# The last two batches in three blocks of 512 tokens instead of four of 384, with PSUM and SBUF shared out anew

## The chip, the cores and the metric

The kernel runs on one core of a Trainium2 chip. The core has a matrix engine (TensorE, "PE" in the profile, with its weight loads as "PEld"), a vector engine (DVE), a scalar engine for activation functions (ACT), a general engine (POOL) and a sequencer that issues the transfers (SP). Matmul results land in PSUM, eight banks of 128 x 512 float32; everything else lives in SBUF. The metric is device microseconds of one execution, the median of several runs.

## The reference

Queries, keys and values have 4 batches, 8 heads, 768 positions and 64 dimensions per head. Each query attends to the keys less than 16 positions away, and to 24 pooled keys: the maximum of the keys over blocks of 32 positions, with log(32) added to their scores and the mean of the block's values as their value. The result, 3072 tokens x 512, goes through a gated feed-forward layer with 1536 hidden columns:

```python
k_sum = k.reshape(B, H, nb, block, D).max(axis=3)
v_sum = v.reshape(B, H, nb, block, D).mean(axis=3)
scores_l_m = np.where(mask_l, scores_l, -1000000000.0)
scores_all = np.concatenate([scores_l_m, scores_s], axis=-1)
a = softmax(scores_all)
x = a @ np.concatenate([v, v_sum], axis=2)       # 3072 x 512 after the heads are joined
out = (silu(x @ w_gate) * (x @ w_val)) @ w_out
```

The weights arrive as 64-bit floats; the kernel turns each into two parts, high and low, of the matrix engine's rounded float32.

## The kernel before

**Blocks.** The 3072 tokens are cut into eight blocks `k` of `TOK` = 384, two per batch, and the eight heads into four pairs `u`. Attention works on one unit (k, u) at a time, in tiles of 64 queries (`QT`): six of them, with windows of 96 keys and the 24 pooled ones, 120 columns (`KC`). The feed-forward layer works on one block and one slice `j` of 128 hidden columns at a time, twelve slices per block.

**One unit of attention.** `a_load` brings the keys of a batch (only in the batch's first block), the queries, the windows of keys (`kw`), and the values for pooling; `a_load_values` the windows of values (`vw`). `a_keys` takes the maximum over key blocks (DVE, L284) and copies it beside the windows (POOL, L154). `a_pool_values` sums the values (DVE, L305) and `a_values` turns the sum by a transpose (PE, L320), scales it (ACT, L321) and copies it beside the value windows (DVE). `a_scores` (L364) does the score matmuls into two PSUM banks, one per head of the pair. `a_exp` is a DVE step that adds the mask and finds the maximum (L408), and the exponential on ACT (L423) with its sum; `a_norm` divides (DVE L440, L441, then POOL L445). `a_transpose` turns the probabilities on PE (L460) and copies them out of PSUM (`pt`, by DVE and ACT). `a_out` multiplies them with the values (L487); `a_split` and `a_rest` cut the result into a high part `xh` (ACT) and a low part `xl` (DVE).

**One slice of the feed-forward layer.** `m_up` (L522) does the gate and then the val product, each as four pairs of heads times three terms (low weight x high input, high x low, high x high), 12 matmuls with 384 moving columns each, into one PSUM bank. `m_silu` (ACT, L528) reads the gate's bank, `m_mul` (DVE, L533) the val's. `m_high` and `m_low` split the product into `ah` (ACT) and `al` (POOL, L148). `m_down` (L572) has the product as weights and `w_o` as 512 moving columns: three terms for each 128 tokens, nine matmuls, accumulated over all twelve slices in one bank per 128 tokens. After the last slice each accumulator is copied to a tile `o` (three buffers) by ACT or DVE in turn and written out.

**Banks and buffers.** PSUM is shared out as two banks for gate and val (`psg`), three for attention (`ps3[0]`, the "a" banks; the first block's accumulators use them too), three for the accumulators (`ps3[1]`). Queries, windows, value windows and probabilities have two buffers each.

**Order.** The first two blocks, with the decoding of the weights, are a list written out by hand (`PROLOGUE`), and their order on each engine is fixed. From slice 6 of block 1 on, the order in the program is: gate, val, and the down product of the slice before. Between these lie numbered places, three per slice, in which the steps of the attention of the next block are put (`put_attention`), each step at a distance from the unit's own place, one unit per nine places. Instructions of this part are only tied to the end of the hand-written list: a planner, which simulates the engines, issues in the order of the program what its cost model holds ready, so a load, a reduction or a copy goes ahead of its written place where its buffer is free. In the trace PE keeps the written order there; loads and the reductions of keys run well ahead.

```python
        m_gate(k, j)
        do(3 * n)
        m_val(k, j)
        do(3 * n + 1)
        if prev:
            m_down(*prev)
        do(3 * n + 2)
```

Of the kernel before, what the change touches and what calls it, by code (L numbers as in the profile page):

```python
# [31 lines left out]
NBLK = B * HALVES  # L32
# [95 lines left out]
def body(ctx, tc, qP, kP, vT, vP, kq, q1, vE, vR, vO, wgv, wo, cst_in, out):  # L128
# [10 lines left out]
    stg = pool("stg", 2)  # L139
# [5 lines left out]
    ps3 = [pool(f"ps{i}", 3, space=bass.MemoryType.PSUM) for i in "ab"]  # L145
# [75 lines left out]
    banks = {"g": psg, "a": ps3[0], "b": ps3[1]}  # L221
# [4 lines left out]
    def a_load_keys(k, u):  # L226
        kt = stg.tile([P, PADS], F32, tag="stg", name=f"kt_{k}_{u}")
        nc.sync.dma_start(kt[:, :PADS], kP[k // HALVES, u])
        KT[u] = kt

    def a_load_queries(k, u):
        b, hf = divmod(k, HALVES)
# [11 lines left out]
    def load_second():  # L244

        t = pro.tile([P, NP, TOK], F32, name="q1")
        nc.sync.dma_start(t, q1)
        for u in range(NP):
            U.setdefault((1, u), {})["q"] = t[:, u]

    def a_load_windows(k, u):
        b, hf = divmod(k, HALVES)
        kw = att.tile([P, NT, KC], F32, tag="kw", name=f"kw_{k}_{u}")
        src = kP[b, u]
        nc.sync.dma_start(
            kw[:, :, :KW], bass.AP(src.tensor, src.offset + hf * TOK, [[PADS, P], [QT, NT], [1, KW]])
        )
        U.setdefault((k, u), {})["kw"] = kw

    def a_load(k, u):  # L260

        b, hf = divmod(k, HALVES)
        if hf == 0:
            a_load_keys(k, u)
        a_load_queries(k, u)
        a_load_windows(k, u)
        if hf == 0:
            vt = stg.tile([P, PADS], F32, tag="stg", name=f"vt_{b}_{u}")[:, :S]
            nc.sync.dma_start(vt, vT[b, u])
            VT[u] = vt  # L270

    def a_load_values(k, u):
        b, hf = divmod(k, HALVES)
        vw = att.tile([KC, NT, P], F32, tag="vw", name=f"vw_{k}_{u}")
        src = vP[b]
        nc.sync.dma_start(
            vw[:KW],
            bass.AP(src.tensor, src.offset + hf * TOK * DM + u * P, [[DM, KW], [QT * DM, NT], [1, P]]),
        )
        U.setdefault((k, u), {})["vw"] = vw  # L280

    def a_pool_keys(u):
        ks = one.tile([P, NB], F32, tag=f"ks{u}", name=f"ks_{u}")
        nc.vector.tensor_reduce(  # L284
            out=ks, in_=KT[u][:, WIN : WIN + S].rearrange("p (n j) -> p n j", j=BLK), axis=AX.X, op=ALU.max
        )
        ksum[u] = ks

    def a_join_keys(k, u):

        copy(
            "p",
            U[k, u]["kw"][:, :, KW:],
            ksum[u].rearrange("p (o n) -> p o n", o=1).broadcast_to([P, NT, NB]),
        )

    def a_keys(k, u):
        if k % HALVES == 0:
            a_pool_keys(u)
        a_join_keys(k, u)  # L300

    def a_pool_values(k, u):
        if k % HALVES == 0:
            vr = att.tile([P, NB], F32, tag="vr", name=f"vr_{k}_{u}")
# [8 lines left out]
    def a_values(k, u):  # L313

        b, hf = divmod(k, HALVES)
        if hf == 0:
            if u == 0:
                vsum["all"] = one.tile([KC, DM], F32, tag="vs", name=f"vs_{b}")
            pv = a_bank(k, u, "pv")
            nc.tensor.transpose(pv[:NB, :P], vsum[u], id_sb)  # L320
            nc.scalar.mul(vsum["all"][KW:, u * P : (u + 1) * P], pv[:NB, :P], 1.0 / BLK)  # L321
        copy("d", U[k, u]["vw"][KW:], pooled(u).broadcast_to([NB, NT, P]))
# [76 lines left out]
    def a_max(k, u, g):  # L399

        t = U[k, u]
        if g == 0:
            t["p"] = (att if k else pro).tile([P, NT, KC], F32, tag="p", bufs=2 if k else 3, name=f"p_{k}_{u}")
            t["nm"], t["sm"], t["ri"] = (sml.tile([P, NT], F32, tag=x, name=f"{x}_{k}_{u}") for x in ("nm", "sm", "ri"))
        for c in range(NT // 2):
            i = g * NT // 2 + c
            n = k % HALVES * NTP + c
# [3 lines left out]
                in1=bias_sb[:, 0 if n == 0 else 2 if n == HALVES * NTP - 1 else 1, :],  # L411
# [7 lines left out]
    def a_half_exp(k, u, g):  # L419
        t = U[k, u]  # L420
        for c in range(NT // 2):
            i = g * NT // 2 + c
# [20 lines left out]
    def a_scale(k, u):  # L443
        p, ri = U[k, u]["p"], U[k, u]["ri"]
        (nc.vector if on == "d" else nc.gpsimd).tensor_tensor(  # L445
            out=p,
            in0=p,
            in1=ri.rearrange("p (n o) -> p n o", o=1).broadcast_to([P, NT, KC]),
            op=ALU.mult,
        )  # L450
# [5 lines left out]
    def a_turn(k, u, g):  # L456
        ps = U[k, u][f"pp{g}"] = a_bank(k, u, f"pp{g}", on[:1] or "a")
        zeros(ps, on[1:])
        for c in range(NT // 2):
            nc.tensor.transpose(ps[:KC, c * P : (c + 1) * P], U[k, u]["p"][:, g * NT // 2 + c, :], id_sb)  # L460

    def a_turned(k, u, g):
        t = U[k, u]
        if "pt" not in t:
            t["pt"] = (one if k else pro).tile([KC, 2, TOK], F32, tag="pt", bufs=1 if k else 2, name=f"pt_{k}_{u}")
        copy(on or "da"[g], t["pt"][:, g, :], t[f"pp{g}"][:KC, :TOK])
# [6 lines left out]
    def a_out(k, u):  # L473
# [3 lines left out]
        for i in range(NT):  # L477
# [19 lines left out]
    def a_split(k, u):  # L497
        ps = U.pop((k, u))["xo"]
        xh = att.tile([P, TOK], F32R, tag=f"xh{u}", name=f"xh_{k}_{u}")
        xl = att.tile([P, TOK], F32R, tag=f"xl{u}", name=f"xl_{k}_{u}")  # L500
        copy(on or "a", xh, ps[:, :TOK])
        X[k, u] = (xh, xl, ps)

    def a_rest(k, u):
        xh, xl, ps = X[k, u]
        subtract("d", xl, ps[:, :TOK], xh)
# [5 lines left out]
    def m_up(k, j, nm, pairs=range(NP)):  # L512
# [5 lines left out]
        for u in pairs:  # L518
            xh, xl = X[k, u]
            cs = slice(u * P, (u + 1) * P)  # L520
            for n, (w, x) in enumerate(((wl, xh), (wh, xl), (wh, xh))):
                nc.tensor.matmul(  # L522
                    ps[:, :TOK], w[:, cs], x, start=u == 0 and n == 0, stop=u == NP - 1 and n == 2
                )

    def m_silu(k, j):
        a = mlp.tile([P, TOK], F32, tag="a", name=f"a_{k}_{j}")
        nc.scalar.activation(out=a, in_=A.pop(("g", k, j))[:, :TOK], func=AF.Silu)  # L528
        A[k, j] = a

    def m_mul(k, j):
        a, ps = A[k, j], A.pop(("v", k, j))
        nc.vector.tensor_tensor(out=a, in0=ps[:, :TOK], in1=a, op=ALU.mult)  # L533

    def m_high(k, j):
        a = A[k, j]
        ah = mlp.tile([P, TOK], F32R, tag="ah", name=f"ah_{k}_{j}")
# [3 lines left out]
    def m_low(k, j):  # L541
        ah, a = A[k, j]
        al = mlp.tile([P, TOK], F32R, tag="al", name=f"al_{k}_{j}")
# [19 lines left out]
    def m_down(k, j):  # L563
        if j == 0:
# [3 lines left out]
        for i in range(NTP):  # L568
# [6 lines left out]
            if j == NJ - 1:  # L575
                o = mlp.tile([P, DM], F32, tag="o", bufs=3, name=f"o_{k}_{i}")
                r = k * TOK + i * P

                parts = 2 if k == NBLK - 1 and i == NTP - 1 else 1
# [20 lines left out]
    def load_consts():  # L600
        nonlocal bias_sb, id_sb, mean_sb
        c = cst.tile([P, 3 * KC + P + NV * QC], F32, name="consts")
        nc.sync.dma_start(c, cst_in)
        bias_sb = c[:, : 3 * KC].rearrange("p (v c) -> p v c", v=3)
        id_sb = c[:, 3 * KC : 3 * KC + P]
        mean_sb = c[:, 3 * KC + P :].rearrange("p (v n) -> p v n", v=NV)
# [11 lines left out]
    def next_room(n):  # L618
        nonlocal pro
# [4 lines left out]
        else:  # L624
            close_pool("dec")
            wts.append(pool("wts3", 1, reuse_waits="tile"))

    bias_sb = id_sb = mean_sb = None
    dec = open_pool("dec", 2, side="right")
# [42 lines left out]
    outs = []  # L672

    def put_attention(k, places, **more):
        steps = dict(
            load=-8, load_values=-4, keys=-3, pool_values=-2, scores=0, exp=0, norm=2, values=2, transpose=4, out=5,
            split=5, rest=5,
        )
        for u, place in enumerate(places):
            for n, x in (steps | more).items():  # L680
                if k == 2 and u == NP - 1:
                    x -= n in ("transpose", "out", "split", "rest")

                if k > 2 and n in ("load", "keys", "pool_values", "scores", "exp"):
                    x += outs[-1] - place
                if (n, k, u) != ("load", 2, 0):
                    put(max(0, place + x), step[n], k, u)
                if n == "out":
                    outs.append(place + x)
# [74 lines left out]
```

## Time and profile before

| | us |
|---|---|
| median of 3 runs (709.41 to 709.81) | 709.42 |
| the profiled execution, its own time | 709.2 |
| its span, first to last instruction | 707.4 |
| PE busy | 701.9 |
| ACT busy | 308.0 |
| DVE busy | 281.7 |
| POOL busy | 137.0 |
| transfers, share of 16 engines' span | 26.2% |

The span is what the profile covers; the execution's own time is 1.8 us more. Engine rows give start and length in us, then engine, line, operation, output and inputs, shapes and count; what stands in square brackets or behind "idle" is how long the engine stood idle before and what ended it. Rows of grouped instructions give the group's busy time and the mean ns of one. A matmul's length holds its way through the array, so successive ones overlap; the distance of their starts tells what one costs. In the chain of waits each row is a start, a length, and the work on the chain.

### The profile page before, as it was taken

To read this page: it belongs to the slowest core of one execution; us is meant where nothing else is said; L and a number is where in the kernel's file an instruction comes from. 1 tells how busy PE (TensorE), PEld (TensorE's weight loads), DVE (VectorE), ACT (ScalarE), POOL (GpSimd) and SP (SyncE) were. 2 spreads that over 40 slices of the span, in tenths; PEclk is the share of its full clock that TensorE was granted. 3 is DMA by queue.
4 is the path that set the end of the run, shared out by engine and by line. 5 is a ranking of instruction groups with operands and counts; after the bars stand their busy time and mean duration, and the time that the engine had idled before them with its cause. 6 is when DMAs were issued, how large, how long until landed. Compare 5 with 4: busy or idle time off the path is not lost.

```text
span 707.4 us, 12740 instructions
## 1 busy us (share of the span) xinstructions
PE 701.9 (99%) x5116; PEld 639.8 (90%) x5116; DVE 281.7 (40%) x822; ACT 308.0 (44%) x765; POOL 137.0 (19%) x143
## 2 busy tenths in 40 slices
PE   9999999999999999999999999999999999999997
PEld 6799999998889999999999999999999999999997
DVE  6999899856642222232332122232223221210001
ACT  6975443327754434344444344443345442421111
POOL 2400120003322221222221222212222212211110
PEclk9999999999999999999999999999999999999999
DMA  9998001146642110222331211120111200010001
GB/s 343 343 419 340 1 1 54 50 136 200 181 141 68 45 45 25 89 68 69 91 88 64 52 45 45 45 90 6 41 46 45 90 18 1 1 45 0 1 1 44
DMA packets 48967, 61.58 MB, mean 87 GB/s; under 512 B 20956, under 2 KB 38108, under 8 KB 47628
## 3 DMA queue, kind: packets, MB, share of 16 engines
q1 hardware_dynamic: 48908, 60.77, 26.2%
q8 instruction: 40, 0.66, 0.4%
q14 instruction: 19, 0.16, 0.1%
HBM read 54.17 MB, written 6.29 MB: 85 GB/s over the span
## 4 chain that ended last, share of the span: by engine, by line
PE 99%; DMA 1%; DVE 0%; SPq 0%; ACT 0%; issue 0%
PE v L522 29%; PE g L522 29%; PE acc L572 28%; PE xo L487 4%; PE pp L460 3%; PE sc L364 3%; PE sc L394 1%; DMA kq<-in_kq 1%; PE sc L380 1%; PE xo L495 0%; PE sc L591 0%; PE pv L338 0%; PE pv L320 0%; PE sc L389 0%; DVE o L154 0%; SPq L240 0%
## 5 line engine op out<-in xcount | busy, mean ns | idle before, releaser
L522 PE MATMUL v<-xh,w_gv 128*128 128x384 f32 x640 | 179.6, 342 | 0.0
L572 PE MATMUL acc<-w_o,ah 128*128 128x512 f32 x576 | 178.9, 392 | 0.0
L522 PE MATMUL g<-xh,w_gv 128*128 128x384 f32 x640 | 178.6, 340 | 0.0
L533 DVE TENSOR_TENSOR a<-v,a 128x384 f32<-128x384 f32 x96 | 53.4, 556 | 252.6 <-PE v L522 250.1
L148 POOL TENSOR_TENSOR al<-a,ah 128x384 fp32r<-128x384 f32 x81 | 83.1, 1026 | 312.6 <-ACT ah L152 297.1
L572 PEld LDWEIGHTS acc<-w_o,ah 128*128 128x128 f32 x576 | 108.0, 188 | 19.9
L522 PEld LDWEIGHTS v<-xh,w_gv 128*128 128x128 f32 x640 | 117.1, 188 | 3.5 <-issue 2.4
L522 PEld LDWEIGHTS g<-xh,w_gv 128*128 128x128 f32 x640 | 117.3, 188 | 2.5 <-ACT a L528 0.4
L572 PE MATMUL acc<-w_o,al 128*128 128x512 f32 x288 | 113.6, 394 | 0.0
L528 ACT ACTIVATE a<-g 128x384 f32<-128x384 f32 x96 | 47.1, 490 | 148.6 <-PE g L522 144.7
L522 PE MATMUL g<-xl,w_gv 128*128 128x384 f32 x320 | 108.0, 338 | 0.0
L522 PE MATMUL v<-xl,w_gv 128*128 128x384 f32 x320 | 107.9, 337 | 0.0
L152 ACT CAST ah<-a 128x384 fp32r<-128x384 f32 x95 | 48.5, 511 | 122.5 <-DVE a L533 114.2
L423 ACT ACTIVATE p<-p,nm 128x120 f32<-128x120 f32 x192 | 73.3, 383 | 7.3 <-DVE nm L408 7.0
L445 POOL TENSOR_TENSOR p<-p,ri 128x720 f32<-128x720 f32 x31 | 43.4, 1400 | 110.6 <-DVE ri L441 105.9
L572 PEld LDWEIGHTS acc<-w_o,al 128*128 128x128 f32 x288 | 54.0, 188 | 9.5 <-issue 0.6
L522 PEld LDWEIGHTS g<-xl,w_gv 128*128 128x128 f32 x320 | 60.1, 188 | 2.2
L522 PEld LDWEIGHTS v<-xl,w_gv 128*128 128x128 f32 x320 | 60.1, 188 | 0.3
L528 ACT ACT_TABLE_LOAD x25 | 32.1, 1283 | 52.9 <-PE g L522 52.7
L408 DVE CUSTOM_DVE_ANT_0 p<-sc,consts 128x120 f32<-128x120 f32 x192 | 41.5, 277 | 2.1 <-PE pp L460 1.0
L522 PE MATMUL g<-xh,w_g 128*128 128x384 f32 x128 | 36.9, 343 | 0.0
L522 PE MATMUL v<-xh,w_v 128*128 128x384 f32 x128 | 36.8, 343 | 0.0
(94 smaller groups left out, 676.0 us busy)
## 6 DMA issues: line engine op xcount, KB each, us to landing
raw_gv<-in_wgv SPq DMA_DIRECT2D x10, 1024.0 KB, 14.6
kw<-in_kP SPq DMA_DIRECT2D x24, 288.0 KB, 3.9
vw<-in_vP SPq DMA_DIRECT2D x24, 288.0 KB, 3.3
raw_o<-in_wo SPq DMA_DIRECT2D x12, 512.0 KB, 13.8
out<-o SPq DMA_DIRECT2D x23, 256.0 KB, 2.3
kt<-in_kP SPq DMA_DIRECT2D x12, 400.0 KB, 3.7
q<-in_qP SPq DMA_DIRECT2D x24, 192.0 KB, 3.4
vt<-in_vT SPq DMA_DIRECT2D x12, 384.0 KB, 3.6
```

The source lines that it names most:

```text
L148: (nc.vector if e == "d" else nc.gpsimd).tensor_tensor(out=out, in0=a, in1=b.bitcast(F32), op=ALU.subtract)
L152: nc.scalar.copy(out, in_)
L364: nc.tensor.matmul(sc[h][s * QT : (s + 1) * QT, c * KC : (c + 1) * KC], t["q"][hs, qs], t["kw"][hs, i, :], start=True, stop=True,)
L408: nc.vector.tensor_tensor_reduce(out=t["p"][:, i, :], in0=t["sc"][g][:, c * KC : (c + 1) * KC], in1=bias_sb[:, 0 if n == 0 else 2 if n == ...
L423: nc.scalar.activation(out=t["p"][:, i, :], in_=t["p"][:, i, :], func=AF.Exp, scale=-1.0, bias=t["nm"][:, i : i + 1], accum_out=t["sm"][:, ...
L445: (nc.vector if on == "d" else nc.gpsimd).tensor_tensor(out=p, in0=p, in1=ri.rearrange("p (n o) -> p n o", o=1).broadcast_to([P, NT, KC]), ...
L460: nc.tensor.transpose(ps[:KC, c * P : (c + 1) * P], U[k, u]["p"][:, g * NT // 2 + c, :], id_sb)
L487: nc.tensor.matmul(ps[hs, qs], vw, t["pt"][:n, h, qs], start=k not in OWN or i == 0, stop=k not in OWN)
L522: nc.tensor.matmul(ps[:, :TOK], w[:, cs], x, start=u == 0 and n == 0, stop=u == NP - 1 and n == 2)
L528: nc.scalar.activation(out=a, in_=A.pop(("g", k, j))[:, :TOK], func=AF.Silu)
L533: nc.vector.tensor_tensor(out=a, in0=ps[:, :TOK], in1=a, op=ALU.mult)
L572: nc.tensor.matmul(ACC[k][i], a[:, ts], w, start=j == 0 and n == 0, stop=j == NJ - 1 and n == 2)
```

## The change

The first four blocks (batches 0 and 1) stay at 384 tokens. The other 1536 tokens become three blocks of 512: `SIZES` lists the widths, `START` the first tokens, and `parts_of(k)` tells which batches a block covers. Block 4 is the first 512 positions of batch 2, block 5 the rest of batch 2 and the first 256 positions of batch 3, block 6 the rest of batch 3. Loads and joins of pooled keys and values go by parts; batch 3 begins in the middle of block 5.

A wide block has eight tiles of 64 queries per unit, 512 columns in the up products, and four accumulators. PSUM: the three accumulator banks stay; when the first wide block begins its down products, the three attention banks are closed and become one bank for the fourth accumulator (`psx`) and two for attention (`psy`). For blocks 5 and 6 the second head's scores go to the two banks of gate and val. SBUF: keys, queries, windows, values, probabilities and their transposes of blocks 2 and up move to a pool `two`, opened where the decoding's buffers are closed, with two buffers for keys and pooled values and one for each of the others. The probabilities and transposes of block 1 move to the pool of the hand-written part. The places of block 2's units become 1, 5, 9 and 12 (they were 4, 7, 10, 13), and the distances of loads and joins are written out. The weights that pool the first batch's values move from the transfer of constants to the next one, that of block 1's queries.

```diff
+WIDE = 512
+NW = WIDE // QT
+SIZES = (TOK,) * (2 * HALVES) + (WIDE,) * ((B - 2) * S // WIDE)
+START = [sum(SIZES[:k]) for k in range(len(SIZES))]
+NBLK = len(SIZES)
+FIRST_WIDE = 2 * HALVES
...
+def parts_of(k):
+    found, at = [], START[k]
+    while at < START[k] + SIZES[k]:
+        b, pos = divmod(at, S)
+        n = min(S - pos, START[k] + SIZES[k] - at)
+        found.append((b, pos, (at - START[k]) // QT, n // QT))
+        at += n
+    return found
...
-    stg = pool("stg", 2)
...
-    ps3 = [pool(f"ps{i}", 3, space=bass.MemoryType.PSUM) for i in "ab"]
+    psb = pool("psb", 3, space=bass.MemoryType.PSUM)
...
-        q = att.tile([P, TOK], F32, tag="q", name=f"q_{k}_{u}")
-        nc.sync.dma_start(q, qP[b, u][:, hf * TOK : (hf + 1) * TOK])
+        q = two.tile([P, WIDE], F32, tag="q", name=f"q_{k}_{u}")
+        for b, pos, i, n in parts_of(k):
+            nc.sync.dma_start(q[:, i * QT : (i + n) * QT], qP[b, u][:, pos : pos + n * QT])
...
     def a_scores(k, u):
         t = U[k, u]
-        sc = [a_bank(k, u, f"sc{h}") for h in range(2)]
-        for i in range(NT):
+        sc = [a_bank(k, u, f"sc{h}", "ag"[h] if k > FIRST_WIDE else "a") for h in range(2)]
+        for i in range(SIZES[k] // QT):
...
         for u in pairs:
...
-                    ps[:, :TOK], w[:, cs], x, start=u == 0 and n == 0, stop=u == NP - 1 and n == 2
+                    ps[:, : SIZES[k]], w[:, cs], x, start=u == 0 and n == 0, stop=u == NP - 1 and n == 2
...
     def m_down(k, j):
+        m = SIZES[k] // P
         if j == 0:
-            ACC[k] = [ps3[1 if k else 0].tile([P, DM], F32, tag="b", name=f"acc{i}_{k}") for i in range(NTP)]
+            if k == FIRST_WIDE:
+                close_pool("psa")
+                banks["x"] = pool("psx", 1, space=bass.MemoryType.PSUM, reuse_waits="tile")
+                banks["a"] = pool("psy", 2, space=bass.MemoryType.PSUM, reuse_waits="tile")
+            ACC[k] = [
+                banks["x" if i == NTP else "b" if k else "a"].tile([P, DM], F32, tag="b", name=f"acc{i}_{k}")
+                for i in range(m)
+            ]
...
         else:
             close_pool("dec")
             wts.append(pool("wts3", 1, reuse_waits="tile"))
+            two = pool("two", 1, reuse_waits="tile")
...
-    def put_attention(k, places, **more):
+    def put_attention(k, u, place, **more):
         steps = dict(
-            load=-8, load_values=-4, keys=-3, pool_values=-2, scores=0, exp=0, norm=2, values=2, transpose=4, out=5,
+            load=-12, load_values=-4, keys=-7, pool_values=-6, scores=-4, exp=-4, norm=2, values=2, transpose=4, out=5,
             split=5, rest=5,
         )
...
-    put_attention(2, (4, 7, 10, 13), load=-5, load_values=-1)
+    early = dict(scores=0, exp=0)
+    put_attention(2, 0, 1, **early, load_values=-1, keys=-1, pool_values=-1)
+    put_attention(2, 1, 5, **early, load=-4, load_values=1, keys=-2, pool_values=-1, values=3)
+    put_attention(2, 2, 9, **early, load=-4, load_values=1, keys=-2, pool_values=-1, values=3, transpose=3)
+    put_attention(2, 3, 12, **early, load=-3, load_values=2, keys=-1, pool_values=0, values=4)
     for k in range(3, NBLK):
-        put_attention(k, [3 * NJ * (k - 2) - 18 + 9 * u + 1 for u in range(NP)])
+        for u in range(NP):
+            place = 3 * NJ * (k - 2) - 18 + 9 * u + 1
+            put_attention(k, u, place, **(dict(load=-7, keys=-5, scores=-2, exp=-2, load_values=-2) if (k, u) == (3, 0) else {}))
```

More of the change, by code (lines that the diff above doesn't have):

```diff
@@ L272, in a_load_values, with a_pool_keys @@
     def a_load_values(k, u):
[L273 to L279, printed above, removed]
+        vw = two.tile([KC, NW, P], F32, tag="vw", name=f"vw_{k}_{u}")
+        for b, pos, i, n in parts_of(k):
+            src = vP[b]
+            nc.sync.dma_start(
+                vw[:KW, i : i + n], bass.AP(src.tensor, src.offset + pos * DM + u * P, [[DM, KW], [QT * DM, n], [1, P]])
+            )
         U.setdefault((k, u), {})["vw"] = vw
-    def a_pool_keys(u):
+    def a_pool_keys(u, lead=WIN):
         ks = one.tile([P, NB], F32, tag=f"ks{u}", name=f"ks_{u}")
         nc.vector.tensor_reduce(
-            out=ks, in_=KT[u][:, WIN : WIN + S].rearrange("p (n j) -> p n j", j=BLK), axis=AX.X, op=ALU.max
+            out=ks, in_=KT[u][:, lead : lead + S].rearrange("p (n j) -> p n j", j=BLK), axis=AX.X, op=ALU.max
         )
         ksum[u] = ks
[L289 to L295, printed above, removed]
-    def a_keys(k, u):
-        if k % HALVES == 0:
-            a_pool_keys(u)
-        a_join_keys(k, u)
+    def a_keys(k, u):
+        for b, pos, i, n in parts_of(k):
+            if pos == 0:
+                a_pool_keys(u, 0)
+            copy(
+                "p",
+                U[k, u]["kw"][:, i : i + n, KW:],
+                ksum[u].rearrange("p (o n) -> p o n", o=1).broadcast_to([P, n, NB]),
+            )
     def a_pool_values(k, u):
-        if k % HALVES == 0:
-            vr = att.tile([P, NB], F32, tag="vr", name=f"vr_{k}_{u}")
+        if any(pos == 0 for b, pos, i, n in parts_of(k)):
+            vr = two.tile([P, NB], F32, tag="vr", name=f"vr_{k}_{u}")
             nc.vector.tensor_reduce(
@@ L313, in a_values @@
     def a_values(k, u):
[L315 to L322, printed above, removed]
+        for b, pos, i, n in parts_of(k):
+            if pos == 0:
+                if u == 0 and i == 0:
+                    vsum["all"] = one.tile([KC, DM], F32, tag="vs", name=f"vs_{b}")
+                pv = a_bank(k, u, "pv")
+                nc.tensor.transpose(pv[:NB, :P], vsum[u], id_sb)
+                nc.scalar.mul(vsum["all"][KW:, u * P : (u + 1) * P], pv[:NB, :P], 1.0 / BLK)
+            copy("d", U[k, u]["vw"][KW:, i : i + n], pooled(u).broadcast_to([NB, n, P]))
     def v_rows():
@@ L401, in a_max @@
         t = U[k, u]
+        m = SIZES[k] // P
         if g == 0:
[L403 to L407, printed above, removed]
+            if k < HALVES:
+                t["p"] = pro.tile([P, NT, KC], F32, tag=f"p{k}", bufs=3 - k, name=f"p_{k}_{u}")
+            else:
+                t["p"] = two.tile([P, NW, KC], F32, tag="p", name=f"p_{k}_{u}")[:, : 2 * m]
+            t["nm"], t["sm"], t["ri"] = (
+                sml.tile([P, NW], F32, tag=x, name=f"{x}_{k}_{u}")[:, : 2 * m] for x in ("nm", "sm", "ri")
+            )
+        for c in range(m):
+            i = g * m + c
+            n = (START[k] // P + c) % (S // P)
             nc.vector.tensor_tensor_reduce(
@@ L420, in a_half_exp @@
         t = U[k, u]
-        for c in range(NT // 2):
-            i = g * NT // 2 + c
+        for i in range(g * SIZES[k] // P, (g + 1) * SIZES[k] // P):
             nc.scalar.activation(
@@ L458, in a_turn @@
         zeros(ps, on[1:])
-        for c in range(NT // 2):
-            nc.tensor.transpose(ps[:KC, c * P : (c + 1) * P], U[k, u]["p"][:, g * NT // 2 + c, :], id_sb)
+        m = SIZES[k] // P
+        for c in range(m):
+            nc.tensor.transpose(ps[:KC, c * P : (c + 1) * P], U[k, u]["p"][:, g * m + c, :], id_sb)
     def a_turned(k, u, g):
@@ L464, in a_turned @@
         if "pt" not in t:
-            t["pt"] = (one if k else pro).tile([KC, 2, TOK], F32, tag="pt", bufs=1 if k else 2, name=f"pt_{k}_{u}")
-        copy(on or "da"[g], t["pt"][:, g, :], t[f"pp{g}"][:KC, :TOK])
+            if k < HALVES:
+                t["pt"] = pro.tile([KC, 2, TOK], F32, tag=f"pt{k}", bufs=2 - k, name=f"pt_{k}_{u}")
+            else:
+                t["pt"] = two.tile([KC, 2, WIDE], F32, tag="pt", name=f"pt_{k}_{u}")
+        copy(on or "da"[g], t["pt"][:, g, : SIZES[k]], t[f"pp{g}"][:KC, : SIZES[k]])
     def a_transpose(k, u):
@@ L476, in a_out @@
         n = KW if k in OWN else KC
-        for i in range(NT):
+        for i in range(SIZES[k] // QT):
             for h in range(2):
@@ L618, in next_room @@
     def next_room(n):
-        nonlocal pro
+        nonlocal pro, two
         if n == 0:
@@ L626, in next_room @@
             wts.append(pool("wts3", 1, reuse_waits="tile"))
+            two = pool("two", 1, reuse_waits="tile")
     bias_sb = id_sb = mean_sb = None
+    banks["a"] = open_pool("psa", 3, space=bass.MemoryType.PSUM)
     dec = open_pool("dec", 2, side="right")
@@ L670, in put @@
         at.setdefault(place, []).append((f, *a))
-    outs = []
-    def put_attention(k, places, **more):
+    def put_attention(k, u, place, **more):
         steps = dict(
-            load=-8, load_values=-4, keys=-3, pool_values=-2, scores=0, exp=0, norm=2, values=2, transpose=4, out=5,
+            load=-12, load_values=-4, keys=-7, pool_values=-6, scores=-4, exp=-4, norm=2, values=2, transpose=4, out=5,
             split=5, rest=5,
         )
[L679 to L689, printed above, removed]
-    put_attention(2, (4, 7, 10, 13), load=-5, load_values=-1)
+        for n, x in (steps | more).items():
+            if (n, k, u) != ("load", 2, 0):
+                put(place + x, step[n], k, u)
+    early = dict(scores=0, exp=0)
[3 more added lines that the diff above has]
+    put_attention(2, 3, 12, **early, load=-3, load_values=2, keys=-1, pool_values=0, values=4)
     for k in range(3, NBLK):
-        put_attention(k, [3 * NJ * (k - 2) - 18 + 9 * u + 1 for u in range(NP)])
+        for u in range(NP):
+            place = 3 * NJ * (k - 2) - 18 + 9 * u + 1
+            put_attention(k, u, place, **(dict(load=-7, keys=-5, scores=-2, exp=-2, load_values=-2) if (k, u) == (3, 0) else {}))
     def do(place):
@@ L750 @@
         "wo": np.ascontiguousarray(wo.reshape(NJ, P, DM)),
-        "consts": np.concatenate([x.reshape(P, -1) for x in (score_bias(), np.eye(P, dtype=np.float32), value_pool())], axis=1),
+        "consts": np.concatenate([x.reshape(P, -1) for x in (score_bias(), np.eye(P, dtype=np.float32))], axis=1),
     }
```

77 lines of the change are left out of this document (39 added, 38 removed).

## The prediction

> **What bounds the kernel now.** I read the page first (busy time per engine and the 40 slices), then the list of what TensorE (PE) waited for, then the chain of waits.
>
> ```profile
> span 707.4 us, 12740 instructions
> ...
> PE 701.9 (99%) x5116; PEld 639.8 (90%) x5116; DVE 281.7 (40%) x822; ACT 308.0 (44%) x765; POOL 137.0 (19%) x143
> ...
> PEclk9999999999999999999999999999999999999999
> ```
> ```profile
> PE warm L591 <- DVE warm L632: 1.4, 1, 1.4
> PE sc L380 <- DMA kq<-in_kq: 0.2, 1, 0.2
> ```
>
> The second fence is all that PE waited for: 1.6 us at the very start. Of the span, 707.4 - 701.9 = 5.5 us is not PE: those 1.6 us and a tail of 3.9 us. Since the page warns that a busy PE need not be at its peak, I looked at the distances from one matmul to the next. In the last block, which has no attention beside it, the chain of waits restricted to that stretch repeats one pattern per 128 hidden columns (start us, us, what):
>
> ```profile
> 645.00 2.11 PE g L522 x12
> 647.11 2.11 PE v L522 x12
> 649.22 2.08 PE acc L572 x9
> ...
> 688.97 2.12 PE g L522 x12
> 691.09 2.12 PE v L522 x12
> 693.21 2.04 PE acc L572 x9
> 695.25 2.12 PE g L522 x12
> ```
>
> From 645.00 to 695.25 there are eight patterns: 50.25 / 8 = 6.28 us each. The nine down matmuls (512 columns) take 2.04 to 2.08 us, 2.06 in the middle, so 229 ns each; the 24 up matmuls (384 columns) take the remaining 4.22 us, 176 ns each. The straight line through the two has (229 - 176) / 128 = 0.414 ns per column and 17 ns that do not depend on the columns. So the kernel is a queue of PE instructions without holes at a granted clock of 1.00, and the only ways to change its time are a different amount of PE work, a hole that opens in it, or its two ends.
>
> **The change part by part.**
>
> *Up projections (L522).* Per block there are 12 x 2 x 4 x 3 = 288 up matmuls, whatever its width. The last 1536 tokens have 4 x 288 = 1152 of 384 columns now and will have 3 x 288 = 864 of 512. The trace has no up matmul of 512 columns. From above, its cost is bounded by pure proportion, 176 x 512/384 = 235 ns; the nearest row is the down matmul, with the same 512 columns, 128x128 weights and three terms, at 229 ns; from below by 227 ns (2.04 us / 9). 1152 x 0.176 = 202.8 us becomes 864 x 0.229 = 197.9 us: -4.9 us, with -6.6 and +0.3 as bounds. The middle of the rows is uncertain by 1 ns, which is 0.9 us here, and I take -4.6. The down projection keeps its count: three matmuls of 512 columns per 128 tokens and 128 hidden columns.
>
> A rule of the Trainium skill (TensorE: Matmul & The Clock Gate, section "Wait — 56ns, not 53.3ns?") speaks against this term: it gives back-to-back matmuls N / 2.4 GHz plus only about 2.5 ns. By it 288 fewer matmuls would be worth 288 x 2.5 ns = 0.7 us. It would put 512 columns at 215.8 ns, and the down rows above have 229 ns, so the trace does not agree with its constant in this stream of paired weight loads.
>
> *Attention on PE.* A unit (one pair of heads of one block) is 6 transposes, 24 output and 24 score matmuls now, 8, 32 and 32 in a wide block. One unit in PE's timeline, and two points four units apart in the chain (same place of the pattern):
>
> ```profile
> 404.26 0.82 PE L460 MATMUL pp<-consts,p 128*120 128x128 f32 x6
> 404.83 0.42 PE L522 MATMUL g<-xh,w_gv 128*128 128x384 f32 x1
> 405.09 0.34 PE L522 MATMUL g<-xl,w_gv 128*128 128x384 f32 x1
> ...
> 407.12 0.92 PE L487 MATMUL xo<-pt,vw 120*64 120x64 f32 x24
> 407.97 0.85 PE L364 MATMUL sc<-kw,q 64*64 64x120 f32 x24
> 408.74 0.44 PE L522 MATMUL v<-xh,w_gv 128*128 128x384 f32 x1
> ```
> ```profile
> 387.43 2.31 PE v L522 x12
> 472.86 2.31 PE v L522 x12
> ```
>
> A block with four units beside it takes 85.43 us against 12 x 6.28 = 75.4: 2.5 us per unit. By the starts, six transposes take 0.57 us, 24 outputs 0.85, 24 scores 0.77, together 2.19; the other 0.3 us is the slower matmul at each change of kind (the first g after the transposes starts 0.26 us before the next, not 0.176). If everything but that 0.3 grows by a third, a wide unit is 2.5 + 0.73 = 3.23 us; twelve of them are 38.8 against sixteen old ones at 40.0: -1.2. But the 0.57, 0.85 and 0.77 hold a fixed part of their own, since a last matmul's drain is in each; with all of it fixed but the bare steps in between, I estimate some 3.1 us and -2. I take -1.6, bounds 0 (all proportional) and -2.2.
>
> *The end.* A wide block ends with four output tiles, and the pool of `o` still has three buffers, so the fourth copy must wait until the first tile has gone out.
>
> ```profile
> 702.25 0.59 ACT L152 COPY o<-acc 128x512 f32<-128x512 f32 x1 [1.54 <-PE acc L572]
> ...
> 702.86 2.11 SPq L583 DMA_DIRECT2D out<-o  x4
> 702.93 0.69 DVE L154 COPY o<-acc 128x512 f32<-128x512 f32 x1 [1.63 <-PE acc L572]
> ...
> 703.61 0.37 ACT L152 COPY o<-acc 128x256 f32<-128x256 f32 x1 [0.77 <-PE acc L572]
> ```
> ```profile
> DMA to landing us min/median/max: 2.0/2.0/2.1
> ```
>
> Copies of one accumulator follow the next at 0.68 us (702.25, 702.93, 703.61), three matmuls of 229 ns. The first copy ends 0.59 us after its start and its transfer lands 2.0 later: 2.65 us after the start with the issue. The fourth accumulator would be copied 3 x 0.68 = 2.04 us after the first. So the last copy starts about 0.7 us late: +0.7 (0.5 to 1.0). In the earlier wide blocks the same wait falls on ACT or DVE while PE goes on with the next block's ups, two of them at 12 x 0.229 = 2.75 us before an accumulator is wanted again.
>
> *Work that I cost at nothing, and its cover.* Silu, product, casts and subtraction grow by a third in columns and occur a quarter less often; the constants' table of pooling weights moves from one early transfer to the one after it, with the same bytes in front of everything later. The tightest chain is in the block before the first wide one: wide attention (eight exponentials) beside a 384 pattern of 6.28 us. The unit at 408 on the other engines:
>
> ```profile
> 407.29 0.49 ACT L528 ACTIVATE a<-g 128x384 f32<-128x384 f32 x1 [1.69 <-PE g L522]
> ...
> 408.58 1.28 ACT L423 ACT_TABLE_LOAD   x1
> ...
> 415.37 1.28 ACT L528 ACT_TABLE_LOAD   x1 [2.71 <-PE g L522]
> ```
> ```profile
> 412.84 1.39 POOL L445 TENSOR_TENSOR p<-p,ri 128x720 f32<-128x720 f32 x1 [3.60 <-DVE ri L441]
> 414.18 1.01 POOL L148 TENSOR_TENSOR al<-a,ah 128x384 fp32r<-128x384 f32 x1
> ```
> ```profile
> L423 ACT ACTIVATE p<-p,nm 128x120 f32<-128x120 f32 x192 | 73.3, 383 | 7.3 <-DVE nm L408 7.0
> ...
> L408 DVE CUSTOM_DVE_ANT_0 p<-sc,consts 128x120 f32<-128x120 f32 x192 | 41.5, 277 | 2.1 <-PE pp L460 1.0 <-PE sc L394 0.5 <-PE sc L364 0.3
> ```
>
> `al` is done at 415.2 and wanted by the down matmuls that follow val (408.74), down, gate and val: 408.74 + 2.2 + 3 x 2.1 = 417.2. Slack 2.0 us. Two more exponentials are 2 x 73.3 / 192 = 0.76, a third of the normalisation 0.46: 0.8 us of slack is left, and if it is gone, `al` late stops PE for the difference, at most four times. In the wide blocks the pattern is 3 x 2.75 = 8.25 us, and the slack is larger.
>
> *Shared PSUM banks.* From the second wide block on, one score bank comes out of the two that gate and val alternate in. The scores are issued right after a gate, so the val behind them needs the gate's bank back, that is, the silu. Cover: silu took 0.49 (0.65 at 512 columns), while the outputs and scores between take 0.85 + 0.77 plus a third, 2.1 us. The next gate needs the scores read by DVE, eight steps of 41.5 / 192 = 0.22 us, and comes two groups (5.5 us) later. Cost 0; without the outputs as cover, see the third rival.
>
> *The second batch's attention*, moved ahead, with one buffer instead of two for queries, windows, values and probabilities. A load can only start when the scores before it are done.
>
> ```profile
> kw<-in_kP SPq DMA_DIRECT2D x7, 288.0 KB, 4.3
> ```
> ```profile
> 160.00 0.85 PE L364 MATMUL sc<-kw,q 64*64 64x120 f32 x24
> ...
> 182.60 0.92 PE L487 MATMUL xo<-pt,vw 120*64 120x64 f32 x24
> ...
> 197.44 0.92 PE L487 MATMUL xo<-pt,vw 120*64 120x64 f32 x24
> ```
> ```profile
> 199.14 2.30 PE g L522 x12
> ```
>
> Scores to next scores is then at least 4.3 us of landing plus some 1 us of issue, and the 0.85 of the scores: 6.2. The first scores move up by a gate and a val (4.2 us) to about 155.8, so the fourth could come at 155.8 + 3 x 6.2 = 174.4. The order puts them in the place where the third unit's outputs stand now, near 182.6. The probabilities' buffer turns once per read by DVE (six times 0.22), table load (1.28), six exponentials (2.3), scaling (1.4) and transposes (0.6), with the hand-overs some 7.5 us, so the fourth scores can come at 155.8 + 22.5 = 178.3. So both chains fit; I take 0, bounds -0.5 (three of the transposes now stand beside scores and save a change of kind) and +4.
>
> **Sum:** -4.6 - 1.6 + 0.7 = -5.5 on the profiled execution, 709.2 us with its span of 707.4: 703.7. The median shown is 709.42, 0.2 above, so 703.9; I say 704.0.
>
> **The rivals.**
>
> 1. *The fixed 17 ns do not belong to the instruction.* If an up matmul costs by its columns alone (235 ns), the first term is gone: 709.4 - 1.6 + 0.7 = 708.5. For it: no up row of 512 columns exists. Against it: up and down have the same form and lie on one line with the same offset. The Trainium skill's constant of 2.5 ns, named above, would give nearly this: 707.8.
>
> 2. *Holes in the second batch.* The single buffers make the four units slip, and the first gate of that block, which needs all four, waits: the last unit's outputs came at 197.44 and the gate at 199.14. A slip of 1 us per unit costs up to 3 us after the small slack: 707. For it: loads and the reductions on keys share DVE with the products that release val's bank. Against it: the 4 us and more of slack above.
>
> 3. *The other side: the gate's bank is missed in every unit of the last two blocks' attention.* Eight units. If the planner issues scores without the outputs before them, or the silu there has to load its table first (1.28, as at 415.37), val waits for 1.28 + 0.65 + latency - 1.0 of scores, about 1 us, and all that follows with it: 8 us, 704.0 + 8 = 712. It decides from 5.5 / 8 = 0.7 us per unit. For it: two banks for three users. Against it: the silu at 407.29 has no table load ahead of it, because the one before it brought the table back.
>
> **How the numbers follow.** A change under 0.2% (1.4 us) cannot be told from none here. Forecast 0.65, first rival 0.07, second (with partial holes of other kinds, 705.5 to 708) 0.19, third 0.09. The likeliest one's own range is 702.3 to 705.5 by the bounds of its terms; taking in the second, 702.3 to 707.6. Faster: the forecast, most of the second, and a part of the first, 0.87; within 0.2%: 0.05; slower 0.08.
>
> **What would show it.** 864 up matmuls with 512 columns in the last blocks, twelve of them in 2.75 us (2.82 under the first rival); PE's list of waits as short as before; a block with wide attention of 99 + 12.5 us; a last copy of `o` that waits for a transfer. A wait of PE for ACT's silu or DVE's scores after 400 us speaks for the third rival, one near 199 us or before it for the second; waits of over 3 us in sum would make the prediction wrong.

## The result and the profile after

| | before | changed |
|---|---|---|
| median of runs on the same chip, us | 709.41 (709.28 to 709.81, 4 runs) | 701.38 (701.05 to 701.71, 4 runs) |
| profiled execution: its own time, us | 709.2 | 701.71 |
| its span, us | 707.4 | 699.9 |

The ratio is 0.9886 (95% interval 0.9869 to 0.9903): 8.0 us faster. The forecast was 704.0 with a range from 702.3 to 707.6; the time lies 0.9 us below that range. The profiled spans differ by 7.5 us only: the profiled execution of before lies 0.2 us under its median, that of the changed kernel is the longest of its four runs. The account below is one of the spans.

From the page of the changed kernel (the span; busy time, share and instructions of TensorE, PE; the granted clock in 40 slices):

```profile
span 699.9 us, 12044 instructions
...
PE 694.0 (99%) x4828; PEld 600.5 (86%) x4828; DVE 278.3 (40%) x795; ACT 292.1 (42%) x724; POOL 134.0 (19%) x127
...
PEclk9999999999999999999999999999999999999999
```

The list of what PE waited for has one row (total, times, longest, in us):

```profile
PE warm L623 <- DVE warm L665: 1.5, 1, 1.5
```

So it is what it was, a queue of PE instructions without holes at the full granted clock, with 288 fewer of them (5116 - 4828). The chain of waits in the last block, where no attention runs beside (start, duration, what):

```profile
592.11 2.72 PE acc L604 x12
594.83 2.72 PE g L546 x12
597.55 2.72 PE v L546 x12
600.27 2.72 PE acc L604 x12
...
690.02 3.42 PE acc L604 x15
```

Every group of twelve takes 2.72 us. From 592.11 to 690.02 there are twelve patterns of 36 matmuls: 97.91 / 432 = 226.6 ns each, up and down alike. The pattern of before was 6.28 us, and four of those did the work of three of these: 25.1 us have become 24.5.

**Where the time went.** One row of the stage windows each, first of before, then of the changed kernel (stretch; its length and the busy time of PE, then PEld, DVE, ACT and POOL; clock; DMA share; GB/s). They are cut at the first gate of block 2, at the first gate of block 4 (the first wide one) and at the end of the last matmul:

```profile
199.10:370.30 171.20, 171.20 (x1233) 157.40 (x1229) 50.46 (x186) 77.19 (x197) 37.04 (x41) 1.00 0.25 71
370.30:703.57 333.27, 333.27 (x2222) 308.00 (x2220) 69.71 (x245) 120.17 (x288) 67.39 (x69) 1.00 0.12 35
```
```profile
200.50:374.30 173.80, 173.80 (x1312) 159.82 (x1309) 53.81 (x205) 81.44 (x217) 39.08 (x42) 1.00 0.28 79
374.30:695.46 321.16, 321.16 (x1854) 264.72 (x1852) 65.39 (x203) 99.54 (x228) 62.62 (x52) 1.00 0.12 36
```

And from the chain the first scores of block 1 and the first gate of block 0, before and changed:

```profile
9.24 0.66 PE sc L380 x24
...
33.48 0.72 PE g L522 x3
```
```profile
9.87 0.66 PE sc L395 x24
...
34.11 0.73 PE g L546 x3
```

| stretch | before | changed | difference |
|---|---|---|---|
| start to the first gate of block 0 | 33.5 | 34.1 | +0.6 |
| to the first gate of block 2 | 165.6 | 166.4 | +0.8 |
| blocks 2 and 3 | 171.2 | 173.8 | +2.6 |
| the last 1536 tokens | 333.3 | 321.2 | -12.1 |
| last matmul to the end of the span | 3.8 | 4.4 | +0.6 |
| sum | 707.4 | 699.9 | -7.5 |

The +2.6 are the four wide units of attention that now run beside block 3 in place of narrow ones. In the last stretch 48 patterns of 6.28 us (301.4) became 36 of 8.16 (293.8): -7.7 for the products alone. What remains of the -12.1, that is -4.4, is attention, and with the +2.6 all attention of the last two batches comes to -1.8. One wide unit in the chain:

```profile
387.55 2.72 PE acc L604 x12
390.28 0.87 PE pp L481 x8
391.15 2.75 PE g L546 x12
393.90 1.08 PE xo L511 x32
394.98 0.98 PE sc L379 x32
395.96 2.95 PE v L546 x12
398.91 2.72 PE acc L604 x12
```

From one acc to the next are 11.36 us, so the unit takes 11.36 - 8.16 = 3.20; twelve of them make 38.4 us, against 40.0 for the sixteen narrow ones of 2.5.

### The profile page after: what moved, and what is told of

It is laid out like the page before. It is cut to its first block, busy times and chain, and to the rows that moved or that the text cites. A ratio compares the mean times of both kernels' runs of the same rounds, so it can differ in the third digit from the quotient of the medians.

```text
span 699.9 us, 12044 instructions
## 1 busy us (share of the span) xinstructions
PE 694.0 (99%) x4828; PEld 600.5 (86%) x4828; DVE 278.3 (40%) x795; ACT 292.1 (42%) x724; POOL 134.0 (19%) x127
## 4 chain that ended last, share of the span: by engine, by line
PE 99%; DMA 0%; ACT 0%; DVE 0%; issue 0%; DVEq 0%
PE v L546 29%; PE g L546 29%; PE acc L604 28%; PE xo L511 4%; PE pp L481 3%; PE sc L379 3%; PE sc L395 1%; PE sc L409 1%; PE warm L623 0%; PE xo L519 0%; PE sc L623 0%; DMA out<-o 0%; PE pv L353 0%; PE sc L404 0%; PE pv L335 0%; ACT o L168 0%
## 5 line engine op out<-in xcount | busy, mean ns | idle before, releaser
L546 PE MATMUL v<-xh,w_gv 128*128 128x384 f32 (+1 forms) x560 | 169.5, 363 | 0.0
L546 PE MATMUL g<-xh,w_gv 128*128 128x384 f32 (+1 forms) x560 | 168.4, 361 | 0.0
L557 DVE TENSOR_TENSOR a<-v,a 128x384 f32<-128x384 f32 (+1 forms) x84 | 51.6, 614 | 250.6 <-PE v L546 242.2
L164 POOL TENSOR_TENSOR al<-a,ah 128x512 fp32r<-128x512 f32 (+1 forms) x69 | 80.7, 1170 | 310.3 <-ACT ah L168 298.9
L552 ACT ACTIVATE a<-g 128x384 f32<-128x384 f32 (+1 forms) x84 | 45.1, 537 | 156.0 <-PE g L546 152.1
L546 PE MATMUL g<-xl,w_gv 128*128 128x384 f32 (+1 forms) x280 | 100.4, 359 | 0.0
L546 PE MATMUL v<-xl,w_gv 128*128 128x384 f32 (+1 forms) x280 | 100.4, 359 | 0.0
L168 ACT CAST ah<-a 128x384 fp32r<-128x384 f32 (+1 forms) x83 | 46.3, 558 | 115.5 <-DVE a L557 107.4
L465 POOL TENSOR_TENSOR p<-p,ri 128x720 f32<-128x720 f32 (+1 forms) x27 | 42.7, 1581 | 89.5 <-DVE ri L461 44.1
L443 ACT ACTIVATION_READ_ACCUMULATOR p<-p,nm 128x1 f32 x192 | 36.1, 188 | 0.0
```

The lines of the kernel that those rows point to most:

```text
L164: (nc.vector if e == "d" else nc.gpsimd).tensor_tensor(out=out, in0=a, in1=b.bitcast(F32), op=ALU.subtract)
L168: nc.scalar.copy(out, in_)
L443: nc.scalar.activation(out=t["p"][:, i, :], in_=t["p"][:, i, :], func=AF.Exp, scale=-1.0, bias=t["nm"][:, i : i + 1], accum_out=t["sm"][:, ...
L465: (nc.vector if on == "d" else nc.gpsimd).tensor_tensor(out=p, in0=p, in1=ri.rearrange("p (n o) -> p n o", o=1).broadcast_to([P, SIZES[k] ...
L546: nc.tensor.matmul(ps[:, : SIZES[k]], w[:, cs], x, start=u == 0 and n == 0, stop=u == NP - 1 and n == 2)
L552: nc.scalar.activation(out=a, in_=A.pop(("g", k, j))[:, : SIZES[k]], func=AF.Silu)
```

## The experiments

**Width alone.** All blocks of 384 tokens again, with everything else of the change left in.

```diff
-SIZES = (TOK,) * (2 * HALVES) + (WIDE,) * ((B - 2) * S // WIDE)
+SIZES = (TOK,) * (B * HALVES)
```

> The changed kernel with eight blocks of 384: the new sharing of PSUM and SBUF, the new places and two attention banks, without the width. Theory (the gain is the width): the up products stay at about 176 ns each, the down products at 230, and the start of the new places costs its 0.8 us in the second batch, so 709.5 to 711.5 us. Rival (part of the gain comes from the new sharing or the new places): clearly below 709.4, 705 to 708 us.

709.19 us (median of 10) beside 709.37 of before (19): ratio 0.9998 (0.9989 to 1.0008), just below the expected 709.5 to 711.5. The gain in time comes with the width; what the new sharing of banks and buffers costs and brings at this width cancels out. In its profile the first gate of block 2 comes as late as in the changed kernel (200.55 us, block 0's at 34.13), so the 0.8 us of the table are there too; against that, the last 1536 tokens take 332.6 us where before has 333.3. The pattern of the last block is nearly the one of before, 6.26 us (the sum of the three groups) against 6.28, and why it is shorter by 0.02 was not tried:

```profile
641.48 2.08 PE v L546 x12
643.56 2.08 PE acc L604 x9
645.64 2.10 PE g L546 x12
```

**What the fixed part of a matmul is.** Two explanations fit the prediction's two points: a fixed time in every instruction, or a bound for the narrow ones alone (their weight load, some 175 ns, the "L" of the expectations). So the last block's gate and val matmuls were cut, first at 256 columns, then at 384:

```diff
-        for u in pairs:
+        cuts = (0, 256, SIZES[k]) if k == NBLK - 1 else (0, SIZES[k])
+        for lo, hi in zip(cuts, cuts[1:]):
+            for u in pairs:
...
-                    ps[:, : SIZES[k]], w[:, cs], x, start=u == 0 and n == 0, stop=u == NP - 1 and n == 2
+                    ps[:, lo:hi], w[:, cs], x[:, lo:hi], start=u == 0 and n == 0, stop=u == NP - 1 and n == 2
```

> The changed kernel; in the last block alone each up matmul of 512 columns is done as two of 256, with the weights loaded for each: 576 instead of 288. Theory L (a matmul cannot start before its weights are in, and that load starts with the matmul before: pitch = the larger of about 175 ns and N/2.4 + 13.3 ns): 576 x 175 = 100.8 us in place of 65.3, so about 737 us, and a pitch of 173 to 177 ns at 256 columns. Rival F (columns plus a fixed part, as the prediction had it): pitch 120 to 124 ns, 576 x 0.122 = 70.3, so about 706 us.

> As the run with halves, but cut at 384 and 128 columns, all matmuls of 384 of a slice ahead of those of 128. Theory L: both at 173 to 177 ns, 576 x 0.175 = 100.8 us, about 737 us. Rival F: 384 at 173 to 177, 128 at 67 to 71, together 245 ns per pair, 288 x 0.245 = 70.6 us, about 706 us.

One run each: 705.48 us with two halves, 718.73 with 384 and 128. The chain of the last block, two halves first:

```profile
645.55 2.87 PE g L548 x24
648.42 2.88 PE v L548 x24
651.30 2.75 PE acc L606 x12
```
```profile
642.40 3.40 PE g L548 x24
645.80 3.43 PE v L548 x24
649.23 2.80 PE acc L606 x12
```

A matmul of 256 columns takes 2.88 / 24 = 120.0 ns. A bound of 175 ns does not exist there, and the halves fall on one line with 226.7 ns at 512: (226.7 - 120.0) / 256 = 0.417 ns per column and 120.0 - 106.7 = 13.3 ns that do not depend on the columns. At 384 that line gives 173.3. With the cut at 384 and 128 the group of 24 takes 3.40; less twelve of 173.3 (2.08), twelve of 128 columns take 1.32, so 110 ns each; in the trace the starts of these matmuls lie 110 to 114 ns apart behind the first. The line would give 66.7, the weight bound 175: neither explanation holds at 128 columns. Something else limits there. A bound of some 111 ns, by the weight load or by another step, would fit all four widths, since 120.0 at 256 columns lies above it; no run tests it.

**Why the pattern of before is longer than its matmuls.** By the line, 24 x 173.3 + 9 x 226.7 ns = 6.20 us, and before has 6.28. In the last two fences the down group is also slower than 2.72 us: 2.75 behind 256 columns, 2.80 behind 128. The explanation tested ("M"): the extra time comes where the width changes. All blocks of 384 again, and the last block's down matmuls write only the first 384 of their 512 output columns; the last 128 output columns of those tokens are left out.

```diff
+DN = lambda k: TOK if k == NBLK - 1 else DM
...
-                    ACC[k][i], a[:, ts], w, start=j == 0 and n == 0, stop=j == NJ - 1 and n == 2
+                    ACC[k][i][:, : DN(k)], a[:, ts], w[:, : DN(k)], start=j == 0 and n == 0, stop=j == NJ - 1 and n == 2
```

> The narrow version (eight blocks of 384), and in the last block the down products take only 384 of the 512 output columns, so that all its matmuls have one width; the last 128 columns of that block are left out. Theory M (N/2.4 + 13.3 ns each, and a transient at every change of width that a block of one width doesn't have): 173.3 ns for nearly every matmul of the last block, 33 x 173.3 = 5.72 us per slice. Rival (384 columns carry their own 2 to 3 ns more): 175 to 177 ns, 5.78 to 5.84 us per slice.

```profile
644.31 2.08 PE g L547 x12
646.39 2.08 PE v L547 x12
648.47 1.56 PE acc L605 x9
```

With one width every matmul takes 173.3 ns (2.08 / 12, 1.56 / 9), and the pattern is 5.72 us, which is 33 x 173.3: nothing is left over. The run differs from the one of width alone by the narrower downs only, and there the pattern is 6.26, 0.06 above the line: 0.04 in the downs (2.08 against 2.04) and 0.02 in the gate behind them (2.10 against 2.08). So 0.06 us of a pattern belong to the change of width. In before it is 0.08, with both up groups at 2.11; no run separates the other 0.02. What in the hardware makes the extra stays open.

**The gate's bank.** In the changed kernel one score bank of a unit comes out of those of gate and val. Here both come out of attention's own two:

```diff
-        sc = [a_bank(k, u, f"sc{h}", "ag"[h] if k > FIRST_WIDE else "a") for h in range(2)]
+        sc = [a_bank(k, u, f"sc{h}", "a") for h in range(2)]
```

> The changed kernel with both heads' scores of blocks 5 and 6 in the two attention banks instead of one in gate's and val's. Theory (the shared bank is what keeps PE without holes): the second scores bank must wait until the outputs' bank has been read by ACT and DVE, about 0.6 + 0.7 us, less what the first scores cover; up to 1 us in each of 8 units, so 703 to 710 us. Rival (the sharing is not needed, and costs something itself): 700.5 to 701.5 us, no wait of PE.

709.59 us (median of 10) beside 709.37 of before: ratio 1.0003 (0.9993 to 1.0012). Without this one line the change brings nothing that can be told. PE's list of waits has no new wait of weight:

```profile
PE warm L623 <- DVE warm L665: 1.5, 1, 1.5
PE sc L395 <- DMA q<-in_q: 0.2, 1, 0.2
```

It is the order. The chain of the unit whose row in the changed kernel is above:

```profile
395.00 0.97 PE sc L379 x16
395.96 0.89 PE v L546 x3
396.86 0.97 PE sc L379 x16
397.82 2.26 PE v L546 x9
400.09 2.72 PE acc L604 x12
```

With a bank missing the planner puts all sixteen scores of one head first, then three val matmuls, then the other head. 32 scores whose heads alternate take 0.98 us, 31 ns each; sixteen of one head take 0.97, 61 ns each. The two heads of a pair lie in different halves of the array's rows (64 each). The Trainium skill (TensorE: Matmul & The Clock Gate, Part 3, "The mechanism") says that matmuls in different row groups run in the array at once; this trace agrees, with 31 against 61 ns. One unit becomes 400.09 - 387.57 - 8.16 = 4.36 us (the acc before it starts at 387.57 here) instead of 3.20, so 1.16 more (0.96 in the scores, the rest in the val group that is now cut in two); seven of the eight units go this way: 8.1 us.

**The end.** The last output tile gets a buffer of the products, which are done by then, instead of waiting for one of the three of `o`.

```diff
-                o = mlp.tile([P, DM], F32, tag="o", bufs=3, name=f"o_{k}_{i}")
+                if k == NBLK - 1 and i == m - 1:
+                    o = mlp.tile([P, WIDE], F32, tag="a", name=f"o_{k}_{i}")
+                else:
+                    o = mlp.tile([P, DM], F32, tag="o", bufs=3, name=f"o_{k}_{i}")
```

> The changed kernel; the very last output tile has a buffer of its own (that of the products) instead of the first tile's. Theory: the last copies no longer wait for a transfer, and the time from the end of the last matmul to the end of the span goes from 4.4 back to 3.8 us. Rival (the end is set by the transfers anyway): 4.4 us as before.

> The version with the last tile's own buffer, timed against the kernel before and, on the same chip, against the changed kernel: 0.6 us below the changed kernel if the shorter tail is all.

> The changed kernel as it is, as the yardstick on the same chip: 701.0 to 701.7 us, and a first gate of block 0 anywhere from 33.3 to 34.1 us if the start differs from run to run and not by the change.

First in one run, 700.28 us, then with rounds beside the changed kernel on the same chip: 700.76 (700.65 to 701.11) against 701.51 (701.29 to 701.67), four runs each, with ratios to before of 0.9882 (0.9866 to 0.9899) and 0.9891 (0.9876 to 0.9906). By the medians the buffer is worth 0.7 us. The end of the changed kernel in the timeline (start, duration, and in brackets the idle time before it and what ended it), and that of the kernel with the buffer:

```profile
695.08 0.39 PE L604 MATMUL acc<-w_o,al 128*128 128x512 f32 x1
696.29 0.42 DVE L170 COPY o<-acc 128x256 f32<-128x256 f32 x1 [1.45 <-DMA out<-o]
```
```profile
694.62 0.39 PE L604 MATMUL acc<-w_o,al 128*128 128x512 f32 x1
695.12 0.42 DVE L170 COPY o<-acc 128x256 f32<-128x256 f32 x1 [0.74 <-PE acc L604]
```

The wait for the transfer is gone: from the start of the last matmul to the copy of the tile's first half are 1.21 us with it and 0.50 without.

**The second batch's attention.** In the changed kernel the scores of block 2 cost more than before:

```profile
163.39 0.66 PE pp L481 x6
164.05 1.40 PE sc L379 x23
...
175.79 1.16 PE sc L379 x24
...
200.55 2.28 PE g L546 x12
```

Before, a unit's 24 scores took 0.78 us:

```profile
160.07 0.78 PE sc L364 x24
```

They now stand right behind the transposes, which hold two of attention's three banks; the third unit's, six val matmuls later, take 1.23. For the three that is 1.45 us more than before. Two remedies were tried. One moves scores and exponentials of three units a step later:

```diff
+    late = dict(scores=1, exp=1)
-    put_attention(2, 1, 5, **early, load=-4, load_values=1, keys=-2, pool_values=-1, values=3)
+    put_attention(2, 1, 5, **late, load=-4, load_values=1, keys=-2, pool_values=-1, values=3)
...
```

> The changed kernel; the scores of units 1 to 3 of block 2 stand one place later, so no longer right behind transposes. Theory (those scores wait for the copies out of the transposes' banks, 0.55 + 0.4 + 0.4 us): the first gate of block 2 comes at about 199.2 us in place of 200.5. Rival (the wait only moves to the outputs or to the next transposes): 200 to 201 us.

> The changed kernel with both edits: the last output tile's own buffer and the later scores in block 2. Theory: 701.4 - 0.6 - 1.3 = 699.5 us. If only the end helps 700.8; if neither 701.4.

It does not help, since the transposes now wait for the scaled probabilities (total, times, longest):

```profile
PE pp L481 <- POOL p L465: 1.7, 2, 0.9
```

The first gate of block 2 comes 167.0 us after block 0's, where the changed kernel has 166.4. One run gave 701.52 us, against 701.38 of the changed kernel. Together with the end buffer it was 701.19 (701.13 to 701.62, four runs; ratio 0.9887, 0.9871 to 0.9904), above the 700.76 of the end buffer by itself on another chip.

The other remedy gives block 2 the shared bank too, with the end buffer left in:

```diff
-        sc = [a_bank(k, u, f"sc{h}", "ag"[h] if k > FIRST_WIDE else "a") for h in range(2)]
+        sc = [a_bank(k, u, f"sc{h}", "ag"[h] if k > FIRST_WIDE or k == 2 else "a") for h in range(2)]
```

> The changed kernel with the last tile's own buffer, and the second head's scores of block 2 too in the banks of gate and val. Theory (block 2's scores wait for the copies out of the transposes' banks): the 24 scores that stand behind transposes take 0.8 us again in place of 1.2 to 1.4, the first gate of block 2 comes 0.5 to 1.3 us earlier after the first gate of block 0 than the changed kernel's 166.5 us, and the time is 0.5 to 1.3 us below that of the version with the buffer alone. Rival (gate and val now wait instead): no gain, or up to 2 us slower.

```profile
163.44 0.66 PE pp L481 x6
164.09 0.78 PE sc L379 x24
...
175.24 0.78 PE sc L379 x24
...
200.07 2.28 PE g L546 x12
```

In these two units the scores are back at 0.78 in the same place behind the transposes, so it was the bank. The third unit gains nothing: its scores now come in two groups of twelve, 0.76 us each, with a down matmul between them. The first gate of block 2 comes at 200.07, not 200.55, with block 0's at 34.1 in both. In the profiles those 0.5 us reach the end: from the first gate of block 0 to the end of the span are 664.6 us with both edits and 665.2 with the end buffer alone. In the times they can't be told: the runs spread from 700.0 to 702.1 (median 700.52, ratio 0.9881, 0.9866 to 0.9896) and overlap with those of the end buffer alone.

## Why the prediction was wrong

What bounds the kernel was read rightly, and so was the sign and the cause of the gain: fewer matmuls, each with a part that does not depend on its width. It was wrong by size: the time came 2.6 us below the forecast and left the range.

- **Up projections** (predicted -4.6, where its own rows gave -4.9; measured -6.7): this is the step that failed, together with the next. 1152 x 175.8 = 202.5 us became 864 x 226.7 = 195.9. The prediction took 229 ns for 512 columns from down matmuls that stand between narrower ones, and a row of 2.04 us (227 ns) as the lower bound. The bound was the true value: the stretch to 229 comes where widths change, and with one width it is gone.
- **Down projection** (predicted 0, "keeps its count"; measured -1.0): the same omission. Its 432 matmuls keep their count, but they fell from 229 to 226.7 ns because their neighbours became as wide as they are. The two together, -7.7, are 288 x 13.3 ns = 3.8 us of fixed parts and 48 patterns at 0.08 us = 3.8 us of extra, of which 0.06 us a pattern is shown to belong to the change of width. The prediction's "17 ns that do not depend on the columns" had mixed these two: the instruction's own part is 13.3. Up to 0.6 us of the last stretch may be the new sharing's and not the width's, since the run of width alone has 332.6 us there against 333.3.
- **Attention** (predicted -1.6; measured -1.8): the bracketing between all-proportional and fixed parts was right; a wide unit takes 3.20 us, where 3.1 to 3.23 were bounds.
- **Block 2's attention** (predicted 0, with -0.5 for transposes beside scores; measured +0.8): the neighbourhood that was counted as a possible saving is a cost, since transposes hold the bank that the scores need to alternate their heads. With another bank for the scores 0.5 of the 0.8 came back; the rest was not followed. The loads and buffers fitted, as reckoned.
- **The end** (predicted +0.7; measured +0.6), shown by the run that removes the wait.
- **Shared banks** (predicted 0): no wait of PE appeared. That is right for the kernel as it is; without the shared bank it is 8.1 us longer, which the prediction did not see.
- **The start** (predicted 0; +0.6): nothing ties it to the change, and the traces show where it arises. From the first scores of block 1 to the first gate of block 0 are 24.24 us in both kernels (9.24 to 33.48, 9.87 to 34.11); the difference lies ahead of them. There the record of the granted clock reaches 1.00 at 5.3 us in the profile of before and at 7.6 in that of the changed kernel, and PE's early score matmuls start 40 ns apart on average until then and 24 afterwards. The transfer that the change made larger, with block 1's queries, lands at 9.06 us where it landed at 9.00. The kernel with the end buffer has the same code up to the last tile; its two profiles reach 1.00 at 5.7 and 6.5 us and have the first gate at 33.3 and 33.7.

Sum of the measured terms: -6.7 - 1.0 - 1.8 + 0.8 + 0.6 + 0.6 = -7.5, as in the spans.

**The rivals.** The first (the fixed part does not belong to the instruction) fell: 256, 384 and 512 columns lie on one line with 13.3 ns. The constant of 2.5 ns in the Trainium skill (TensorE: Matmul & The Clock Gate, "Wait — 56ns, not 53.3ns?") does not hold in this stream either, where each matmul has its own weight load: the trace has 226.7 at 512 columns and not 215.8. The second (holes in the second batch) did not occur as waits. The third (the gate's bank missed, with PE waiting for the silu) did not occur: PE's list has no such wait. That 8 us hang on this bank all the same is a coincidence of size: they are lost when the bank is not shared, through heads that no longer alternate, and that case the prediction did not have.

**The range.** The bounds of the prediction's own terms, -6.6, -2.2 and +0.5, reach to 709.4 - 8.3 = 701.1 and would have held the time. The range ended at 702.3, as if the low ends could not meet. Two of those terms rest on the same unknown, the time that a matmul has beside what its columns take, so their low ends can come together. That the time lies above 701.1 is luck in part: the down projection's -1.0 was in no bound, and block 2's +0.8 made up for most of it.

## What to carry to other kernels

Take the price of an instruction from rows in which its neighbours are like those it will have: a duration read between instructions of another shape holds some of the change between them, and if a change makes neighbours alike, the ones that keep their count get cheaper too. Where matmuls use half of the array's rows in turn, look at the order in which they are issued and not only at waits, since one PSUM bank less can break the alternation and double their time without a single wait in the profile. And where several terms hang on one unknown, add up their low ends for the range.

## What the runs showed of the hardware

- A matmul with its own 128x128 weights takes 0.417 ns per column plus 13.3 ns: 120.0 ns at 256, 173.3 at 384, 226.7 at 512. At 128 columns it is about 110 ns, above that line.
- Where two widths alternate, a pattern of 33 matmuls takes 0.06 to 0.08 us more than the sum of its matmuls; with one width the extra is gone. The cause is open.
- 64-row matmuls of 120 columns take 31 ns each with the array's two halves in turn and 61 ns each in one half.
- The record of the granted clock reaches 1.00 at 4.5 to 7.7 us after the start of the span in the thirteen profiles, though PE's first matmul starts at 1.45 us in all of them. With it, and with the landing of block 1's queries (8.8 to 9.8 us), the first gate of block 0 moves between 33.3 and 34.2 us.
